# Retention, routed experts and a cosine layer on one core: paired scores, capacities by rank, paced transfers, a branch around the overflow turns

## The chip, the cores and the metric

The kernel runs on one core of a Trainium2 chip. The metric is the device time of one execution in microseconds (us), as the median of several runs; lower is better. The engines are TensorE (PE; PEld is its weight load), VectorE (DVE), ScalarE (ACT), GpSimd (POOL) and SyncE (SP), each with its own instruction queue, worked through in order. SP starts most transfers, GpSimd the indirect ones.

## The reference

Three layers follow one another on 4 x 576 = 2304 tokens of 512 columns (8 heads of 64):

```
# 1. retention, per head, gamma = 1 - 2^(-5-h)
scores = q @ k.T / 8;  ret = scores * (gamma ** (i - j) where i >= j else 0);  x = ret @ v
# 2. top 2 of 8 experts; noisy = x @ w_gate + log1p(exp(x @ w_noise)) * noise
w = softmax of the two largest of noisy
out[token] += w_k * (relu(x @ w1[e]) @ w2[e])     # w1 512 x 1024, w2 1024 x 512
# 3. h = out @ w_in (512 x 2048);  result = (h * cos(h)) @ w_out (2048 x 512)
```

q, k, v, the gate and the experts are float32; the last layer's two weights arrive as float64. With the reference's own inputs the experts get 614, 587, 570, 539, 535, 566, 606 and 591 tokens.

## The kernel before

**Retention** goes tile by tile (20 tiles: four of 128 tokens and one of 64 in each batch). For tile j SP loads queries (`qr`), keys (`kb`) and keys and values (`kv`), four tiles ahead (`LOOK`). GpSimd multiplies queries and values by decays (`decay`, L418; `decay_v`, L426), VectorE the first four tiles' queries. `scores` (L444) makes K Q^T for eight heads: `kb` is held in two copies with one head's 64 rows set to zero, so that each matmul uses all 128 rows. VectorE masks the result out of PSUM (L445, two instructions of 128 x 512 a tile). `outputs` (L468 to L487) adds what the running state gives, multiplies with the values, the two heads of a pair on column halves of the array (L473), and renews the state. `gate` and `gate_t` make the routing logits and write the tokens to `xs` in DRAM in 32 x 32 blocks.

**Routing** runs in four groups of tiles (`routing`, a generator): softplus, the two largest, ranks by matmuls with ones, then a table of tokens by slot, built from one-hot tiles (`sa` L645, `sb` L646). `pump` hands its steps to VectorE between the steps of the array, by estimates (`spent`) of what array and VectorE were given so far, always the older group first (`LASTFIRST` is False). Expert 0's first 320 tokens (`CUT0`), known after two groups, are served early: `layer1(0, 0, True)` and `layer2(0, 0, True)` keep the array busy while routing ends (`fill`, and the loop over `post`).

**Experts.** Each has 616 slots (`CAP`), whatever its count; tokens beyond go through `overflow` in plain float32, 128 a turn, in a loop whose number of turns is loaded into registers at run time. Weights come in units of 128 x 1024 through three staging tiles (`load_unit`, SP). `split_unit` takes each into a float32r high part (ScalarE, L288) and a low part (L289, VectorE or GpSimd by lists as `B_POOL`, `SA_POOL`); both layers use three products, high-high, low-high and high-low (`PASSES`; L796 and L817). An expert's columns go in two groups (256 and 360; expert 0: 320 and 296). `gather` fetches the next expert's rows for blocks of 128 tokens by four indirect transfers each (L721, GpSimd), all of them issued ahead of the expert; `turn` transposes them by VectorE in 32 x 32 blocks (L754) and splits them. Results are turned back and go to `ys`. Beside this VectorE turns the float64 weights to float32 by their bits (`conv`, L1116 to L1122), in steps spread by `CG0`, `CG1` and `CG2`.

**Last layer.** Nine blocks of 256 tokens (the last 128 by halves): `fetch` (L1150, sixteen indirect transfers a block), `turn2` (weigh, add, transpose, split), `mlp1` (L1190 to L1208) and `mlp2` (L1220). A block's fetch runs during the block before it; the first block's during the last expert.

The order is written out by hand: the loops at the end of `moe_kernel` say after which step of the array each split, turn, gather and conversion step is put.

Of the kernel before, what the change touches and what calls it, by code (L numbers as in the profile page):

```python
# [10 lines left out]
F32 = mybir.dt.float32  # L11
# [20 lines left out]
# slots of an expert, in two groups: expert 0's and the others'  # L32
CAP = 616
NB = 5
CUT0, CUT = 320, 256
ROOM = (CUT0, CAP - CUT)
XB = (N - 512) // 128
YR = E * CAP
# [7 lines left out]
ZERO = (11, 13, 22, 27, 27, 29, 33)  # L46
LOOK = 4
WJ = 3
T0_AT = ()
GLP = 8  # L50
GLP0 = 4
FS = 1
FS0 = 1
SPP = (0, 3, 6, 9)
SP0 = (0, 1, 2, 3, 4, 5, 6, 7, 8, 9)
CG0 = 4
CG1 = 2
CG2 = 1
SB_AT = (1, 4, 7, 10)
SB_POOL = ()  # L60
SA_POOL = (1, 2, 3, 4, 5, 6)
TURN_AT = (1, 2, 3, 5, 6)
SPLIT_AT = (1, 2, 4, 5)
L_AT = (1, 2, 3, 5, 8, 9, 10, 11, 13, 15)
L_POOL = (2, 4, 7)
T2_AT = (1, 2)
# [6 lines left out]
LASTFIRST = False  # L73
# [3 lines left out]
L_US = 0.04  # L77
# [6 lines left out]
B_AT = (0, 1, 2, 24)  # L84
B_POOL = range(99)
TURN_AT0 = (1, 1, 2, 3, 4)
# [4 lines left out]
# where the last layer's weight units go: 8 of w_in, 8 of w_out  # L91
# [27 lines left out]
def constants():  # L119
# [26 lines left out]
    # counts from which an expert needs one, two, ... turns more  # L146
    xb = np.tile(512 + 128 * np.arange(XB), (E, 1))
    xb[:, 0] = CAP
# [8 lines left out]
    small = np.concatenate([xb, io, base, k[:, None], k[:, None] // 32, tok, it], 1)  # L157
    # k = 32 g + t to 32 a + t, for every a
# [9 lines left out]
SMALL = [("xb", E * XB), ("io", E), ("base", GN * E), ("pi", 1), ("pa", 1), ("tok", NTILE), ("it", E * RB)]  # L168
# [25 lines left out]
    # rows of tokens lie as [32-row of the array, chunk, 32]; expert 0's are turned a 128 at a time  # L194
# [19 lines left out]
def moe_kernel(ctx, tc, x, out, dbg=None, phases="ABC"):  # L214
# [29 lines left out]
    spread = be.tile([128, 4, 128], F32, name="spread")  # L244
    vs = con.tile([128, 2, NTILE], F32, name="vs")
    eix = con.tile([128, 2, NTILE], F32, name="eix")
    oh = con.tile([128, 2, NTILE, E], F32, name="oh")
    gidx = con.tile([128, E * RB], I32, name="gidx")
    egid = con.tile([128, 3], I32, name="egid")
    cnt = con.tile([128, E], F32, name="cnt")  # L250
    ntot = con.tile([128, 1], I32, name="ntot")
    cbias = con.tile([128, 2], F32, name="cbias")
    nc.gpsimd.memset(cbias[:, 0:1], MAGIC)
# [3 lines left out]
    units = []  # L257
    for e in range(E):
        units += [(f"a{j}", x["w1"][4 * (e or E) + j], [128, DC, 256]) for j in range(4)]
        units += [(f"b{j}", x["w2"][4 * e + j], [128, 2, DM]) for j in range(4)]  # L260
# [3 lines left out]
    state.update(load=0, split=0, a=wpa)  # L264
# [4 lines left out]
    def load_unit():  # L269
        u = state["load"]  # L270
        if u >= len(units):
            return
        state["load"] += 1
        st = stage.tile([128, 1024], F32, name="st")
        nc.sync.dma_start(st, units[u][1])
        loaded[u] = st

    def split_unit(lo_engine=nc.vector):
# [13 lines left out]
        load_unit()  # L292

# [8 lines left out]
    # the array's clock rises while it works: it is kept busy until the first data are there  # L302
# [11 lines left out]
    for i in range(LOOK):  # L314
        t = ca.tile([128, HP, 2, 128], F32, name=f"kb{i}")
        eng = nc.gpsimd if i else nc.vector
        eng.memset(t[:64, :, 1, :], 0.0)
        eng.memset(t[64:, :, 0, :], 0.0)
        KB.append(t)
# [10 lines left out]
    def load_k(j):  # L330
        b, c = divmod(j, NC)
        kb, src = (KB[(4 * b + c) % LOOK], x["kt"][4 * b + c]) if c < 4 else (KBT, x["ktt"][b])
        for s in range(2):
            nc.sync.dma_start(kb[s * 64:(s + 1) * 64, :, s, :],
                              src[s * 64:(s + 1) * 64].rearrange("p (a t) -> p a t", a=HP))
        KT[j] = kb
# [44 lines left out]
    adj = rt.tile([128, E], BF, name="adj")  # L381
    ptab = ps.tile([128, E * RB], F32, name="ptab")
    lgs = []
    for i in range(2):
        t = rt.tile([128, GN, 2 * E], F32, name=f"lg{i}")
        lgs.append(t)

    def late_consts():
# [18 lines left out]
        nc.sync.dma_start(spread.rearrange("p a b -> p (a b)"), x["c_spread"])  # L407
# [27 lines left out]
    def scores(j):  # L435
        b, c = divmod(j, NC)
        am = wk.tile([128, HP, 2, 128], F32, name="am", bufs=2)
        if c < 4:
            for h2 in range(2):
                p = ps.tile([128, 2, 2, 128], F32, name="ph", bufs=PHB)  # L440
                for i in range(2):
                    hp = 2 * h2 + i
                    for s in range(2):
                        nc.tensor.matmul(p[:, i, s, :], KT[j][:, hp, s, :], QT[j][:, hp, :], start=True, stop=True)  # L444
                nc.vector.tensor_tensor(  # L445
                    am[:, 2 * h2:2 * h2 + 2].rearrange("p a s q -> p (a s) q"),
                    p.rearrange("p a s q -> p (a s) q"),
                    bs["mask"][:, None, :].to_broadcast([128, 4, 128]), op=OP.mult)
                AM[j] = am
                yield  # L450
# [44 lines left out]
    def gate(j):  # L495
# [9 lines left out]
        # tokens to spread rows, 32 x 32 at a time  # L505
# [19 lines left out]
    def spread_out(src, tag, bufs):  # L525
        """[32 g + t, n] to [32 a + t, g, n] for every a."""
        n = src.shape[-1]
        pq = ps.tile([128, 4, n], F32, name=tag, bufs=bufs)
        for g in range(4):
            nc.tensor.matmul(pq[:, g], spread[:, g], src, start=True, stop=True)  # L530
        return pq

    ranked, begun = [0], []
# [801 lines left out]
```

## Time and profile before

| | |
|---|---|
| median of three runs | 1105.34 us (1099.04 to 1111.32) |
| span of the profiled execution, first to last instruction | 1012.0 us (its time with what lies around is not given) |
| TensorE / its weight loads busy | 970.4 / 912.4 us |
| VectorE / ScalarE / GpSimd busy | 699.4 / 369.6 / 532.1 us |
| mean granted clock of TensorE | 0.988 of full speed |
| moved by DMA | 135.4 MB, 134 GB/s over the span |

Busy times are sums over each engine; the span is longer than any of them. "Idle before" belongs to the instruction behind it, with what ended it in brackets. Granted clock 1.00 is full speed, 2.4 GHz.

### The profile page before, as it was taken

The page shows a single profiled execution, that of the slowest core. Times are in us where ns is not written, and L with a number is a line of the kernel's source. Part 1 is how long each engine was busy: PE and PEld are TensorE (multiplying, and loading weights), DVE is VectorE, ACT ScalarE, POOL GpSimd, SP SyncE. Part 2 cuts the span into 40 slices and gives each one's busy share as a digit, 9 for nine tenths or more (in the row PEclk, how much of TensorE's full clock was granted, in tenths as well). Part 3 has the DMA queues.
Part 4 walks back from the last instruction along what each step waited for, and adds up shares of the span by engine and source line. Part 5 has one row for each costly group of instructions (what it writes and reads, how often), then busy time and mean ns, then how long its engine had stood idle before and what let it go on. Part 6 is the DMA issues. An engine that isn't in the chain of part 4 may idle for free. (4 is left out here: it accounts for less than half of the span.)

```text
span 1012.0 us, 17885 instructions
## 1 busy us (share of the span) xinstructions
PE 970.4 (96%) x6845; PEld 912.4 (90%) x6845; DVE 699.4 (69%) x1337; ACT 369.6 (37%) x657; POOL 532.1 (53%) x467
## 2 busy tenths in 40 slices
PE   8989987989999999999999999899999999999998
PEld 6878777979999999999999998799898989989897
DVE  4698883697989889894444459585665848475671
ACT  2422411242323232233333336353443535354451
POOL 6343333676655647475731447374746456473721
PEclk9999988989999999999999999999999999999999
DMA  9999584275866768484525533101111010111100
GB/s 284 285 268 271 137 276 132 78 230 169 233 234 196 239 205 283 146 281 120 165 87 155 146 94 123 47 25 42 32 37 50 21 50 19 45 29 41 32 22 22
DMA packets 85847, 135.38 MB, mean 134 GB/s; under 512 B 13376, under 2 KB 51648, under 8 KB 85760
## 3 DMA queue, kind: packets, MB, share of 16 engines
q1 hardware_dynamic: 76048, 113.74, 36.5%
q0 software_dynamic: 9568, 20.20, 7.0%
q8 instruction: 55, 0.90, 0.4%
q10 hardware_dynamic: 144, 0.27, 0.1%
q14 instruction: 32, 0.26, 0.1%
HBM read 106.25 MB, written 35.26 MB: 140 GB/s over the span
## 5 line engine op out<-in xcount | busy, mean ns | idle before, releaser
L721 POOL DMA_INDIRECT rows<-xs,gidx x140 | 154.3, 1102 | 55.9 <-issue 46.6
L1150 POOL DMA_INDIRECT y<-ys,slot x144 | 141.0, 979 | 56.0 <-issue 26.1
L1208 POOL TENSOR_TENSOR gl<-t,gh 128x512 fp32r<-128x512 f32 x68 | 88.6, 1303 | 139.7 <-issue 110.1
L289 POOL TENSOR_TENSOR la<-st,ha 128x1024 fp32r<-128x1024 f32 x28 | 69.6, 2492 | 98.3 <-ACT ha L288 98.3
L817 PE MATMUL ph<-hh,lb 128*128 128x360 f32 (+2 forms) x312 | 96.0, 308 | 0.0
L817 PE MATMUL ph<-hl,hb 128*128 128x360 f32 (+2 forms) x312 | 95.9, 308 | 0.0
L817 PE MATMUL ph<-hh,hb 128*128 128x360 f32 (+2 forms) x312 | 95.5, 306 | 0.0
L1169 DVE SCALAR_TENSOR_TENSOR y<-y,wts,y 128x128 f32<-128x128 f32 x72 | 34.8, 511 | 61.6 <-DMA y<-ys,slot 54.6
L1198 DVE TENSOR_SCALAR t<-t 128x512 int32<-128x512 int32 x72 | 73.1, 1016 | 2.5
L1196 DVE TENSOR_SCALAR t<-t 128x512 f32<-128x512 f32 x72 | 37.4, 519 | 50.3 <-ACT t L1195 50.3
L746 ACT ACTIVATE xh<-xt 128x512 fp32r<-128x512 f32 (+1 forms) x35 | 21.5, 616 | 137.8 <-DVE xt L754 137.8
L1201 ACT ACTIVATE t<-t,cbias 128x512 f32<-128x512 f32 x72 | 52.0, 722 | 33.0 <-DVE t L1198 32.0
L1220 PE MATMUL py<-hd,gl 128*128 128x512 f32 (+1 forms) x152 | 57.7, 380 | 1.5 <-DVE gl L1208 1.5
L817 PEld LDWEIGHTS ph<-hh,hb 128*128 128x128 f32 x312 | 58.9, 189 | 0.0
L817 PEld LDWEIGHTS ph<-hl,hb 128*128 128x128 f32 x312 | 58.6, 188 | 0.0
L817 PEld LDWEIGHTS ph<-hh,lb 128*128 128x128 f32 x312 | 58.5, 188 | 0.0
L1220 PE MATMUL py<-hb,gl 128*128 128x512 f32 (+1 forms) x152 | 58.4, 384 | 0.0
L1220 PE MATMUL py<-lb,gh 128*128 128x512 f32 (+1 forms) x152 | 58.4, 384 | 0.0
L1220 PE MATMUL py<-hb,gh 128*128 128x512 f32 (+1 forms) x152 | 58.3, 384 | 0.0
L1220 PE MATMUL py<-hd,gh 128*128 128x512 f32 (+1 forms) x152 | 57.5, 378 | 0.0
L1220 PE MATMUL py<-ld,gh 128*128 128x512 f32 (+1 forms) x152 | 57.5, 378 | 0.0
L796 PE MATMUL ph<-xh,ha 128*128 128x360 f32 (+3 forms) x236 | 45.8, 317 | 6.3 <-DVE hl L802 4.3
(309 smaller groups left out, 2705.5 us busy)
## 6 DMA issues: line engine op xcount, KB each, us to landing
st<-w SPq DMA_DIRECT2D x64, 512.0 KB
kv<-kv SPq DMA_DIRECT2D x16, 512.0 KB
ci<-wi SPq DMA_DIRECT2D x16, 512.0 KB
wc<-cy SPq DMA_DIRECT2D x32, 256.0 KB
ci<-wo SPq DMA_DIRECT2D x16, 512.0 KB
st<-wc SPq DMA_DIRECT2D x16, 512.0 KB
ys<-c_zero SPq DMA_DIRECT2D x7, 1024.0 KB
qr<-qt SPq DMA_DIRECT2D x20, 256.0 KB
```

Source lines behind the costliest of these rows:

```text
L289: lo_engine.tensor_tensor(lo.rearrange("p a b -> p (a b)"), st, hi.bitcast(F32).rearrange("p a b -> p (a b)"), op=OP.subtract)
L721: nc.gpsimd.indirect_dma_start(out=t[:, g, :], out_offset=None, in_=xs.rearrange("n (a d) -> (n a) d", a=4), in_offset=bass.IndirectOffset ...
L746: nc.scalar.activation(hi, src, AF.Copy)
L796: nc.tensor.matmul(p[:, :n], w[a][:, dc, (f % 2) * 128:(f % 2 + 1) * 128], XE[e, g][b][:, dc, :n], start=(i == 0), stop=(i == 3 * DC - 1))
L817: nc.tensor.matmul(p[:, :n], w[a][:, f % 2, c * 128:(c + 1) * 128], HE[e, g][b][:, f, :n], start=(i == 0), stop=(i == 3 * FC - 1))
L1150: nc.gpsimd.indirect_dma_start(out=t[:, g, :], out_offset=None, in_=(ys if i else ys[:FIRST]).rearrange("n (a d) -> (n a) d", a=4), in_off ...
L1169: nc.vector.scalar_tensor_tensor(y0[:, g], y1[:, g], w1, y0[:, g], op0=OP.mult, op1=OP.add)
L1196: nc.vector.tensor_scalar(t, t, -MAGIC, None, op0=OP.add)
L1198: nc.vector.tensor_scalar(t.bitcast(I32), t.bitcast(I32), 0x7FFFFFFF, None, op0=OP.bitwise_and)
L1201: nc.scalar.activation(t, t, AF.Sin, scale=-1.0, bias=cbias[:, 1:2])
L1208: (nc.gpsimd if g < (GLP if i else GLP0) else nc.vector).tensor_tensor(fl(gl), T[g], fl(gh.bitcast(F32)), op=OP.subtract)
L1220: nc.tensor.matmul(ps_[tb][:, :c1 - c0], parts[f // 2][b][:, f % 2, tb * 128:(tb + 1) * 128], w[a][:, f % 2, c0:c1], start=(f + k == 0), s ...
```

## The change

Keys lie in one piece and each head's scores use half of the array's rows, two heads side by side into two PSUM banks. Experts 1 to 7 are served in the order of their counts, with capacities from 616 down to 560 (`CAPS`); expert 0 stays first. For that `rank_experts` sorts counts on VectorE behind the last group's table, and SP loads seven expert numbers into registers; the weights of experts 1 to 7 are addressed by them, and loads asked for before are owed. The last routing group's steps go first, and the end of the earlier groups is put off (`rest`). The two of seven 1 MB zero writes to `ys` that were issued during retention move behind it. Most low parts go from GpSimd to VectorE, at other places. GpSimd takes the gathers one by one, each behind a one-element copy of the array's last result (`pace`). Expert 1's first two blocks and the last layer's first block are fetched as whole rows, one transfer a block and source, and transposed by TensorE. The overflow loop stands in a branch. Expert 0's early group has 352 columns.

```diff
-CAP = 616
+CAPS = (616, 616, 600, 592, 584, 576, 568, 560)
+BASE = tuple(sum(CAPS[:i]) for i in range(E))
-CUT0, CUT = 320, 256
+CUT0, CUT = 352, 256
-ZERO = (11, 13, 22, 27, 27, 29, 33)
+ZERO = (22, 27, 27, 29, 33, 38, 44)
-LASTFIRST = False
+LASTFIRST = True
-L_US = 0.04
+L_US = 0.1
-B_AT = (0, 1, 2, 24)
-B_POOL = range(99)
+B_AT = (0, 5, 10, 24)
...
 def load_unit():
+        if u // 8 < E and u // 8 not in expert:
+            state["owed"] += 1
+            return
...
 def scores(j):
-            for h2 in range(2):
-                p = ps.tile([128, 2, 2, 128], F32, name="ph", bufs=PHB)
-                for i in range(2):
-                    hp = 2 * h2 + i
-                    for s in range(2):
-                        nc.tensor.matmul(p[:, i, s, :], KT[j][:, hp, s, :], QT[j][:, hp, :], start=True, stop=True)
...
+            pp = [ps.tile([128, HP, 128], F32, name="ph", bufs=PHB) for _ in range(2)]
+            for hp in range(HP):
+                for s in range(2):
+                    h = slice(s * 64, s * 64 + 64)
+                    nc.tensor.matmul(pp[s][:, hp, :], KT[j][h, hp, :], QT[j][h, hp, :], start=True, stop=True)
+            for s in range(2):
+                nc.vector.tensor_tensor(am[:, :, s, :], pp[s], bs["mask"][:, None, :].to_broadcast([128, HP, 128]),
+                                        op=OP.mult)
...
+    def rank_experts():
...
+        vec.tensor_copy(cnt, pn)
+        vec.scalar_tensor_tensor(key, cnt, 8.0, sl["tie"], op0=OP.mult, op1=OP.add)
+        vec.tensor_tensor(sq, row(key), column(key), op=OP.is_gt)
+        vec.tensor_reduce(at_, sq, axis=AX.X, op=OP.add)
+        vec.tensor_tensor(hot, row(at_), column(sl["io"]), op=OP.is_equal)
+        vec.tensor_tensor(sq, hot, row(sl["io"]), op=OP.mult)
+        vec.tensor_reduce(order, sq, axis=AX.X, op=OP.add)
+        for e in range(1, E):
+            expert[e] = nc.values_load(order[0:1, e:e + 1], engines=[mybir.EngineType.SP], min_val=1, max_val=E - 1)
+        for _ in range(state["owed"]):
+            load_unit()
...
 def routing(gi):
...
+            yield from rank_experts()
+            vec.tensor_tensor(gs, hot[:, :, None, :].to_broadcast([128, E, NB, E]),
+                              gf.rearrange("p e n -> p n e")[:, None].to_broadcast([128, E, NB, E]), op=OP.mult)
+            vec.tensor_reduce(gf, gs, axis=AX.X, op=OP.add)
+            vec.tensor_copy(whole, gf[:, 1, :WHOLE1])
...
+    def pace(src):
+        nc.gpsimd.tensor_copy(beat, src.bitcast(F32))
...
 def turn(e, blk, early=False):
+            if e:
+                t = bpool[1].tile([128, DC, 128], F32, name="xt")
+                nc.scalar.activation(t.rearrange("p c (a d) -> p c a d", a=4),
+                                     ROWS[e, blk].rearrange("p a (c d) -> p c a d", c=DC), AF.Copy)
             for a in range(4):
-                nc.tensor.transpose(p[:, a, :], ROWS[e, blk][:, a, :], ident)
+                nc.tensor.transpose(p[:, a, :], t[:, a, :], ident)
...
 def pump():
+            elif m == "done" and not l1:
+                gens.remove(it)
+                rest.append(it)
...
-            split_unit(nc.gpsimd if k in B_POOL else nc.vector)
-            if k not in B_POOL:
-                spent(0, B_US)
+            split_unit()
+            spent(0, B_US)
...
 def overflow():
         total = nc.values_load(ntot[0:1, 0:1], min_val=0, max_val=OVB)
-        with tc.tile_pool(name="ov", bufs=1) as ov:
+        with tc.If(total > 0):
+            with tc.tile_pool(name="ov", bufs=1) as ov:
...
 # the order of the experts
+        gq = gathers(e + 1) if e + 1 < E else iter(())
+        if not e:
+            steps(gq, WHOLE1)
...
             for _ in layer1(e, g):
                 n += 1
+                pace(HE[e, g][0][0:1, (n - 1) % FC, 0:1])
+                steps(gq, 2 if last and n < 13 else 1)
...
-                elif state["split"] < 8 * e + 8 and n in SB_AT:
-                    split_unit(nc.gpsimd if n in SB_POOL else nc.vector)
-                if not e or n > CG0 and n % CG1 == 0:
+                elif n in ((*SB_AT, *SA_AT) if e else SA_AT0):
+                    split_unit()
+                if not e or n in CG_1:
                     steps(cg, 1)
...
 # the order of the last layer
             if n in SP0 and state["split"] < len(units):
-                split_unit(nc.gpsimd if n in SPP else nc.vector)
-            steps(fg, FS if i else FS0)
+                split_unit()
+            if not i and parts:
+                pace(parts[-1][0][0:1, 0, 0:1])
+            steps(fg, 1 if i or n > 5 else 2)
```

## Rows read from the trace of the kernel before

**Rows 1.** Busy times by stage: length, engines' busy us (instructions), granted clock, DMA share, GB/s.
```profile
20.00:106.00 86.00, 78.48 (x812) 68.01 (x810) 69.23 (x214) 27.63 (x63) 36.43 (x39) 1.00 0.94 274
...
122.00:168.40 46.40, 35.20 (x241) 32.60 (x240) 30.23 (x113) 9.37 (x19) 12.34 (x7) 0.89 0.63 197
168.40:217.50 49.10, 44.07 (x295) 43.45 (x296) 34.82 (x70) 14.71 (x27) 33.56 (x27) 0.89 0.44 130
217.50:594.00 376.50, 373.76 (x2595) 371.41 (x2593) 275.74 (x471) 121.06 (x205) 210.99 (x158) 1.00 0.60 189
...
645.20:1012.00 366.80, 363.26 (x2352) 332.35 (x2352) 225.57 (x341) 160.70 (x281) 188.18 (x174) 1.00 0.12 34
sum 1012.00, PE 970.40 PEld 912.44 DVE 699.43 ACT 369.65 POOL 532.08; mean PE 121.30 PEld 114.06 DVE 87.43 ACT 46.21 POOL 66.51
```

**Rows 2.** The chain that ended last: start, us, what; 256 columns, then 512.
```profile
645.24 4.38 PE ptab L1190 x24
...
670.00 22.15 PE py L1220 x96
...
697.89 5.76 PE pt L1190 x48
```

**Rows 3.** Timeline of TensorE in one tile of retention: start, us, instruction, count.
```profile
45.50 2.05 PE L444 MATMUL ph<-qt,kb 128*128 128x128 f32 x16 [0.94 <-POOL qt L418]
...
48.93 1.09 PE L473 MATMUL py<-am,vt 128*64 128x128 f32 x16
```

**Rows 4.** Waits of all engines: total us, times, longest.
```profile
POOL qt L418 <- DMA qr<-qt: 37.6, 10, 7.5
```

**Rows 5.** Groups of VectorE's instructions from 20 to 122 us.
```profile
L445 DVE TENSOR_TENSOR am<-ph,cb 128x512 f32<-128x512 f32 x27 | 17.9, 679 | 0.6 <-PE ph L444 0.4
```

**Rows 6.** Timeline of three engines around 130 us.
```profile
125.38 7.04 POOL L289 TENSOR_TENSOR lb<-st,hb 128x1024 fp32r<-128x1024 f32 x3 [10.93 <-ACT hb L288]
130.09 2.38 DVE L645 TENSOR_SCALAR sa<-it,vf 128x128 f16<-128x128 f16 x1
132.62 0.24 DVE L645 TENSOR_SCALAR sa<-it,vf 128x128 f16<-128x128 f16 x1
133.54 1.44 PE L796 MATMUL ph<-xh,ha 128*128 128x320 f32 x4 [4.29 <-DVE hl L802]
137.71 0.91 PE L796 MATMUL ph<-xh,ha 128*128 128x320 f32 x4
```

**Rows 7.** Groups of the whole span: the low parts of weight units.
```profile
L289 POOL TENSOR_TENSOR la<-st,ha 128x1024 fp32r<-128x1024 f32 x28 | 69.6, 2492 | 98.3 <-ACT ha L288 98.3
L289 DVE TENSOR_TENSOR lb<-st,hb 128x1024 fp32r<-128x1024 f32 x29 | 36.2, 1248 | 5.6 <-ACT hb L288 5.3
```

**Rows 8.** Timeline of TensorE behind the overflow loop.
```profile
168.44 1.35 PE L796 MATMUL pt<-xh,ha 128*128 128x296 f32 x4 [6.28 <-DMA ys<-y]
...
172.41 0.71 PE L796 MATMUL pt<-xh,la 128*128 128x296 f32 x4
```

**Rows 9.** Timeline of TensorE at the start of expert 1.
```profile
206.24 1.16 PE L796 MATMUL ph<-xh,la 128*128 128x256 f32 x4 [1.84 <-POOL la L289]
...
209.76 0.65 PE L796 MATMUL ph<-xl,ha 128*128 128x256 f32 x4
...
213.20 1.22 PE L796 MATMUL pt<-xh,ha 128*128 128x256 f32 x4 [2.79 <-DVE hl L802]
```

**Rows 10.** Timeline: expert 0's last gathers on GpSimd, transposes on TensorE.
```profile
152.24 0.95 POOL L726 DMA_INDIRECT rows<-xs,gidx  x1 [0.30 <-issue]
153.49 0.95 POOL L726 DMA_INDIRECT rows<-xs,gidx  x1 [0.30 <-issue]
160.69 1.03 PE L763 MATMUL pt<-ident,rows 128*128 128x128 f32 x8
```

**Rows 11.** Timeline of TensorE in the last layer's first block and behind it.
```profile
630.56 0.50 PE L1220 MATMUL py<-hd,gl 128*128 128x512 f32 x1 [1.51 <-DVE gl L1208]
...
645.24 0.74 PE L1190 MATMUL ptab<-x2h,hc 128*128 128x256 f32 x4 [3.85 <-ACT x2h L746]
```

More of the change, by code (lines that the diff above doesn't have):

```diff
@@ L1 @@
 from contextlib import ExitStack
+from functools import partial
 from itertools import chain
@@ L257, in moe_kernel, with unit @@
     units = []
+    expert = {0: 0}
+    def unit(name, e, j):
+        if not e:
+            return x[name][4 * (E if name == "w1" else 0) + j]
+        return x[name][bass.ds(expert[e] * 4 + j, 1)].rearrange("u p c -> (u p) c")
     for e in range(E):
-        units += [(f"a{j}", x["w1"][4 * (e or E) + j], [128, DC, 256]) for j in range(4)]
-        units += [(f"b{j}", x["w2"][4 * e + j], [128, 2, DM]) for j in range(4)]
+        units += [(f"a{j}", partial(unit, "w1", e, j), [128, DC, 256]) for j in range(4)]
+        units += [(f"b{j}", partial(unit, "w2", e, j), [128, 2, DM]) for j in range(4)]
     wcf = wc.bitcast(F32)
@@ L263, in moe_kernel @@
     loaded, W = {}, {}
-    state.update(load=0, split=0, a=wpa)
+    state.update(load=0, split=0, owed=0, a=wpa)
     def x_tiles(g):
@@ L381, in moe_kernel @@
     adj = rt.tile([128, E], BF, name="adj")
+    hot = rt.tile([128, E, E], F32, name="hot")
+    order = rt.tile([128, E], I32, name="order")
     ptab = ps.tile([128, E * RB], F32, name="ptab")
@@ L386, in moe_kernel, with drain @@
         lgs.append(t)
+    def drain(g):
+        for _ in g:
+            pass
     def late_consts():
@@ L651, in routing @@
         yield "table"
+        while tabled[0] < gi:
+            yield "wait"
+        tabled[0] += 1
         table(0, gi == len(GRP) - 1)
@@ L713, in moe_kernel, with spread_rows, gathers @@
     ROWS, XE, HE, bpool = {}, {}, {}, {0: be}
+    def spread_rows(e, blk):
+        return e > 1 or e == 1 and blk >= WHOLE1
+    def gathers(e):
+        for blk in range(NB):
+            yield from gather(e, blk)
     def gather(e, blk, early=False):
@@ L836, in layer2 @@
         yield
-    gens, clock, early = [], [0], []
+    gens, rest, clock, early = [], [], [0], []
     at = {"P": 0.0, "D": 0.0}
@@ L877, in pump_to @@
                 return
+            elif m == "done" and len(gens) > 1:
+                rest.append(gens.pop(0))
+        for it in rest[::-1]:
+            drain(it[0])
     turned = []
@@ L1146, in fetch @@
             ys12 = []
+            if not i:
+                for kk in range(2):
+                    t = cx.tile([128, 4, 128], F32, name=f"y{kk}", bufs=2)
+                    nc.gpsimd.indirect_dma_start(out=t.rearrange("p a d -> p (a d)"), out_offset=None, in_=ys[:FIRST],
+                                                 in_offset=bass.IndirectOffsetOnAxis(ap=slot0[:, kk, j:j + 1], axis=0))
+                    yield
+                    ys12.append(t)
+                Y12[i].append((j, *ys12))
+                continue
             for kk in range(2):
@@ L1252, in moe_kernel @@
     for e in range(E):
-        if e + 1 < E:
-            for blk in range(NB):
-                gather(e + 1, blk)
+        gq = gathers(e + 1) if e + 1 < E else iter(())
+        if not e:
+            steps(gq, WHOLE1)
         n = 0
@@ L1276, in moe_kernel @@
                     drain(layer2(e, 0))
-                    drain(fetch(0))
+                    gq = fetch(0)
         t2 = turn2(0) if last else iter(())
         m = 0
+        if 0 in T2_AT:
+            steps(t2, 1)
         for _ in chain(layer2(e, 0), layer2(e, 1)) if 0 < e < E - 1 else layer2(e, 1):
             m += 1
+            steps(gq, 2 if last or not e else 1)
             if last:
@@ L1290, in moe_kernel @@
                         turn(e + 1, blk)
-                if m in SPLIT_AT or not e:
-                    split_unit(nc.gpsimd if m in SA_POOL else nc.vector)
-            steps(cg, CG2)
+                if state["split"] < 8 * e + 12:
+                    split_unit()
+            if e and m in CG_2:
+                steps(cg, 1)
         if e == E - 2:
```

353 lines of the change are left out of this document (203 added, 150 removed).

## The prediction

> **What bounds the kernel now.** I read the busy times by stage first, then the chain of waits, then the timeline of TensorE wherever a stage was not full, and last the groups of instructions for the durations. TensorE works 970.4 of 1012.0 us. The stages [rows 1] are retention and gate (20 to 106, running out by 122), the routing of the last tokens with expert 0's early product as filler (to 168.4), expert 0's second group and the start of expert 1 (to 217.5), experts 1 to 7 (to 594), the first block of the last layer (to 645), and the eight other blocks. The expert stage (373.8 of 376.5 us) and the last stage (363.3 of 366.8) are full: there only fewer matmul columns help. The other four lack 7.5, 11.2, 5.0 and, by its two idles [rows 11], 5.4 us, and in two of them the mean granted clock is 0.89: after a long idle TensorE comes back at the lower of its two levels (1.2 instead of 2.4 GHz) for a few us. What is won there is the idle time and the slow stretch behind it. In retention the DMA share is 0.94 while TensorE is 91% and VectorE 80% busy, so three resources are near their end together.
>
> The chain ends in nothing but matmuls of the last layer, so what is saved ahead of them moves the end one to one. The sum is made against the span of the one profiled execution; no time of its own is given for it. The median of the runs, 1105.3 us, is 93.3 above that span; I keep these 93.3.
>
> **The change, part by part.**
>
> *Ranked capacities.* 4,928 expert columns (8 x 616) become 4,712, so 216 fewer. A column passes 192 matmuls (96 in each layer of an expert: 8 x 4 x 3). A matmul of 256 columns takes 5.76/48 = 0.120 us, one of 512 22.15/96 = 0.231 [rows 2], so 0.432 ns a column. 216 x 192 x 0.432 ns = **17.9 us less**, all in the full stage. The bounds are close together: it comes out unless another engine takes over. It holds as long as no expert has more tokens than its slots, since no overflow turn runs before, and by the reference's own inputs the counts (614 for expert 0; then 606, 591, 587, 570, 566, 539, 535) fit the new capacities too.
>
> *Row-tiled scores.* Now 16 instructions with half the rows zero take 2.05 us a tile; the 16 that already go in pairs, on column halves, take 1.09 [rows 3]. If row halves pair as well, TensorE is given back 0.96 us x 16 tiles = 15.4 us; if not, nothing. It is not the only bound: GpSimd waits 37.6 us for the queries' transfers [rows 4], and TensorE then for GpSimd. What DMA gives back is the two 1 MB zero writes that leave this stage: 274 GB/s at a share of 0.94 is 291 at full, so 3.6 us each, 7.2 of 0.94 x 86 = 80.8 us. At the same share the stage then takes 73.6/0.94 = 78.3, 7.7 less. With about 1 us in the two tiles that run out behind it I take **8.5 us less**, between 0 and 15.4. VectorE's 69.2 us then stand in some 78 (88%): tight, but open. Keys in one piece instead of two save SP queue time and eight clears at the start; nothing on the path.
> A rule speaks against this step. VectorE reads the scores of a tile out of PSUM in two pieces of 0.68 us [rows 5], 1.36 us, more than the 1.09 that the paired matmuls would need. The Trainium skill says so in general (TensorEngine Tiling (Array Packing), PSUM Bottleneck): packing speeds up the array but not the emptying of PSUM, which may become the bottleneck. By it a tile would gain 2.05 - 1.36 = 0.69, 11 us in all; still above what the transfers allow, so my term stands.
>
> *Splits off GpSimd, and the order of routing.* At 125.4 GpSimd splits three weight units, 7.04 us. Meanwhile VectorE's routing instructions take up to 2.38 us instead of 0.24, and TensorE waits 4.29 us for VectorE [rows 6]. From there the next twelve matmuls of 320 columns, with four small ones between, take 4.17 us; at 0.148 each and 0.5 for the four it would be 2.3, so 1.9 more. That is 6.2 us. With these splits on VectorE (1.25 us each [rows 7]) and the last group's steps first, most of it goes: **5 less**; ends 6.2 less and, if the four splits fall into the routing chain itself, 5 more. What is late next is that chain; its cover is expert 0's early product, 10% longer now (352 instead of 320 columns, paid back in the second group).
>
> *Overflow in a branch.* The loop of zero turns costs an idle of 6.28 us and a slow stretch, 16 matmuls of 296 columns in 3.97 us [rows 8] where 0.137 each makes 2.2, so 1.8 more: 8.1. The register load and the jump on all engines remain, the loop's entry and exit should not. No row shows a branch alone; between 8.1 less and a second such idle, 6.3 more, I take **3 less**.
>
> *Expert 1.* TensorE idles 1.84 us for GpSimd's split and 2.79 for VectorE there, and 16 matmuls of 256 columns behind the first take 3.52 us [rows 9] instead of 1.92, 1.6 more; I put the same behind the second. That is 7.8 us. Splits earlier and on VectorE, and two blocks gathered as whole rows (1 indirect transfer in place of 4, 1.25 us apart): **5.5 less**.
> Against it stands the ranking: about 15 more VectorE instructions (0.2 to 0.5 us, some 5 us) and seven register loads on SP before any weight of expert 1 is asked for, with SP's queue behind them. The three gathers of expert 0 go out before; now 6 us lie between them and the end of the filler at 160.7 [rows 10], and expert 0's second group (24 us) comes still before expert 1. I take **2 more**; ends 0 and 8.8, seven times the 1.25 us that lie between two indirect transfers on their queue [rows 10], the nearest row to a load that a queue makes itself.
>
> *Last layer's first blocks.* 1.51 and 3.85 us of idle [rows 11]; behind the second 24 matmuls take 4.38 us [rows 2] instead of 2.88, 1.5 more: 6.9. Block 1's sixteen fetches go out two at a step and GpSimd loses its splits: **5 less**; ends 6.9 less, and 2.6 more if the splits on VectorE push its chain.
>
> *Added.* 16 transposes (8 take 1.03 us [rows 10]): **2 more**. One-element copies that pace GpSimd: 0, GpSimd is half idle; if its queue ran behind, expert turns would wait, which the gathers' slack (20 in 24 steps) excludes in the common case.
>
> Sum: -17.9 - 8.5 - 5 - 3 - 5.5 + 2 - 5 + 2 = -40.9. The span becomes 971, the time **1064 us**.
>
> **Rivals.**
> (a) *The ranking takes the place of the waits it stands beside*: steps 3 and 5 give nothing (10.5) and the register loads cost some 8 in front of expert 1. For it: weights can't be prefetched over it. Against: 24 us of cover. 1064 + 18 = 1082.
> (b) *Retention does not shrink*: the row halves do not pair (then the change does not do what it says), or VectorE or the transfers hold the pace. 1064 + 8.5 = 1073.
> (c) *VectorE becomes the bound of the experts*. The 28 splits that the row groups [rows 7] x 1.25 = 35 us come to its 341 us between 122 and 594 [rows 1]: 376 of about 445, 84%, and it loses the blocking by GpSimd. Only bursts could bind. The whole column gain would go: 1064 + 18 = 1082.
> (d) *Slower: TensorE's clock falls in retention.* With 13 us of scores taken out and the transfers as they are, it idles more often. Its price: work at the lower level takes twice as long, so the stage's 65 us of work could cost up to 65 more, 1129. It outweighs the gains from 41 us at the lower level on, that is from two thirds of the stage. Against it: this stage already idles 7.5 of 86 us in pieces and its granted clock is 1.00 [rows 1]; the falls named above follow idles of 1.8 us or more, and TensorE's waits here are of 1.3 at most.
>
> **How the numbers follow.** Forecast 0.62, (a) 0.17, (b) 0.09, (c) 0.06, (d) 0.06. The range takes in (a) to (c) and the better ends, 17.9 + 15.4 + 6.2 + 8.1 + 7.8 + 6.9 - 2 = 60 less, 1045; with some us of the runs' own spread (1099 to 1111) I give 1042 to 1090. One per cent, about what can be told from no change here, is 11 us: below 1094 is faster. That holds in the forecast, (b), and most of (a) and (c): 0.87; the same 0.08; slower 0.05, (d).
>
> **What would show it.** Expert matmuls of 344 down to 304 columns and an expert stage some 15 us shorter with VectorE below 90%; score pairs in 1.1 us a tile; retention's DMA share still above 0.9 with TensorE near 83%; no idle over 2 us before expert 0's late group except at the branch; a first fetch of block 1 done before its block 0 ends. I am wrong if TensorE waits for VectorE in the experts, for the weights of expert 1, or if retention still ends near 122.

## The result and the profile after

The changed kernel takes 956.24 us (954.50 to 959.04, four runs) against 1105.84 (1099.04 to 1111.32, four runs) before: a ratio of 0.868 [0.864, 0.873], 150 us less. Ratios, here and below, are estimated without runs over 1.5% above the fastest of the same kernel, with a 95% interval in brackets, so they need not equal the quotient of two medians. The forecast was 1064, with a range of 1042 to 1090; the sign was right, the size far off. In the profiled execution the changed kernel's span is 954.6 us and its time 956.36, so 1.8 us lie around the span, not the 93.3 that I kept. From span to span the change is worth 57.4 us, where my sum had 40.9.

So there are two questions: what the 93 us were, and where another 16 us of span came from. The page of the kernel after, first lines and three groups (line, engine, operation, count, busy us, mean ns, idle time ahead of them):

```profile
span 954.6 us, 18171 instructions
...
PE 935.2 (98%) x6861; PEld 878.1 (92%) x6861; DVE 676.1 (71%) x1381; ACT 367.8 (39%) x653; POOL 469.2 (49%) x536
...
L811 POOL DMA_INDIRECT rows<-xs,gidx x132 | 135.1, 1024 | 32.4 <-issue 25.3
L824 POOL COPY beat<-hh 1x1 f32<-1x1 f32 x120 | 49.0, 408 | 150.8 <-ACT hh L903 148.3
L311 DVE TENSOR_TENSOR lb<-st,hb 128x1024 fp32r<-128x1024 f32 x35 | 43.7, 1247 | 11.7 <-ACT hb L310 10.5
```

Ahead of the pacing copies GpSimd waits 150.8 us, 148.3 of them for ScalarE, and GpSimd is still only 49% busy. Stages of the kernel after (columns as in [rows 1]):

```profile
20.00:106.00 86.00, 79.80 (x886) 66.91 (x882) 71.12 (x227) 29.26 (x68) 39.26 (x43) 0.94 0.81 251
...
122.00:151.00 29.00, 27.71 (x192) 25.57 (x190) 21.36 (x98) 4.09 (x8) 4.78 (x5) 1.00 0.95 326
151.00:178.00 27.00, 24.79 (x200) 24.40 (x201) 21.18 (x73) 10.10 (x20) 14.55 (x20) 1.00 0.67 200
178.00:217.50 39.50, 39.50 (x298) 39.50 (x297) 28.96 (x51) 16.53 (x28) 24.76 (x36) 1.00 0.63 184
217.50:542.00 324.50, 324.36 (x2410) 324.15 (x2409) 246.41 (x468) 108.31 (x182) 152.63 (x201) 1.00 0.67 202
542.00:590.00 48.00, 46.04 (x291) 41.16 (x290) 38.43 (x59) 26.41 (x43) 29.63 (x30) 1.00 0.36 104
```

From 178 to 542 us TensorE has hardly a gap: the stage that lacked 5 us at expert 1 [rows 1] is full. Most of what is left ahead of the last layer is in retention (clock 0.94) and behind the branch. TensorE's timeline, start, us, instruction, idle before:

```profile
51.55 1.16 PE L478 MATMUL ph<-qt,kb 64*128 64x128 f32 x16
...
57.68 2.15 PE L478 MATMUL ph<-qt,kb 64*128 64x128 f32 x16 [2.12 <-DVE sa L721]
...
113.11 0.75 PE L898 MATMUL ph<-xh,ha 128*128 128x352 f32 x3 [0.27 <-ACT xh L842]
...
151.11 0.72 PE L898 MATMUL pt<-xh,ha 128*128 128x264 f32 x4 [0.43 <-PEq L1087]
...
154.72 0.75 PE L898 MATMUL pt<-xh,ha 128*128 128x264 f32 x4 [1.92 <-ACTq L1087]
...
178.03 0.64 PE L898 MATMUL pt<-xh,ha 128*128 128x256 f32 x4
...
589.88 0.74 PE L1337 MATMUL ph<-x2h,hc 128*128 128x256 f32 x4 [1.42 <-ACT x2h L842]
```

The profile puts the wait ahead of 57.68 down to `sa`, which these matmuls don't read. They read `qt`, and GpSimd made that after a wait for the queries' transfer, ready 0.06 us before they start, so the wait is most likely for that transfer:

```profile
56.36 1.26 POOL L452 TENSOR_TENSOR qt<-qr,dq 128x512 f32<-128x512 f32 x1 [4.13 <-DMA qr<-qt]
```

Read the starts. Expert 0's early product goes on behind the last gate at 113.11 (before 120.80), its late group starts at 151.11 (168.44 [rows 8]), expert 1 at 178.03 (197.38), the last layer at 542.06 (594.07), its block 1 at 589.88 (645.24 [rows 11]). The gains are 7.7, 9.6, 2.0, 32.7 and 3.4 us, and 2.0 in the eight blocks behind. Expert 0's 32 columns that moved from its late to its early group lie in the second and the third of these gains: by 0.432 ns a column they are 2.7 us, against the 9.6 and for the 2.0.

### The profile page after: what moved, and what is told of

Read it like the earlier page. It is cut to its first block, busy times and chain, and to the rows that moved or that the text cites. A ratio compares the mean times of both kernels' runs of the same rounds, so it can differ in the third digit from the quotient of the medians.

```text
span 954.6 us, 18171 instructions
## 1 busy us (share of the span) xinstructions
PE 935.2 (98%) x6861; PEld 878.1 (92%) x6861; DVE 676.1 (71%) x1381; ACT 367.8 (39%) x653; POOL 469.2 (49%) x536
## 4 chain that ended last, share of the span: by engine, by line
PE 79%; DVE 3%; issue 1%; ACT 1%; DMA 1%; DVEq 0%; SPq 0%; ACTq 0%
PE py L1366 19%; PE ph L919 13%; PE ph L1337 11%; PE ph L898 8%; PE pt L1337 7%; PE pt L898 7%; PE pt L919 4%; PE ptab L898 4%; PE ptab L1337 3%; PE ptab L919 3%; DMA st<-w 1%; DVE y L1316 0%; DVE t L1344 0%; DVE t L1349 0%; DVE hl L904 0%
## 5 line engine op out<-in xcount | busy, mean ns | idle before, releaser
L811 POOL DMA_INDIRECT rows<-xs,gidx x132 | 135.1, 1024 | 32.4 <-issue 25.3
L1280 POOL DMA_INDIRECT y<-ys,slot x128 | 125.7, 982 | 50.8 <-issue 21.1
L824 POOL COPY beat<-hh 1x1 f32<-1x1 f32 x120 | 49.0, 408 | 150.8 <-ACT hh L903 148.3
L919 PE MATMUL ph<-hl,hb 128*128 128x256 f32 (+8 forms) x304 | 91.0, 299 | 0.0
L919 PE MATMUL ph<-hh,lb 128*128 128x256 f32 (+8 forms) x304 | 91.0, 299 | 0.0
L919 PE MATMUL ph<-hh,hb 128*128 128x256 f32 (+8 forms) x304 | 90.7, 298 | 0.0
L1343 DVE TENSOR_SCALAR t<-t 128x512 f32<-128x512 f32 x72 | 35.0, 487 | 48.4 <-ACT t L1342 48.4
L1345 DVE TENSOR_SCALAR t<-t 128x512 int32<-128x512 int32 x72 | 67.1, 932 | 2.5
L842 ACT ACTIVATE xh<-xt 128x512 fp32r<-128x512 f32 (+7 forms) x33 | 19.6, 593 | 114.2 <-DVE xt L850 95.3
L1366 PE MATMUL py<-ld,gh 128*128 128x512 f32 (+1 forms) x152 | 57.4, 378 | 0.0
L311 DVE TENSOR_TENSOR lb<-st,hb 128x1024 fp32r<-128x1024 f32 x35 | 43.7, 1247 | 11.7 <-ACT hb L310 10.5
```

The source lines that it names most:

```text
L311: lo_engine.tensor_tensor(lo.rearrange("p a b -> p (a b)"), st, hi.bitcast(F32).rearrange("p a b -> p (a b)"), op=OP.subtract)
L811: nc.gpsimd.indirect_dma_start(out=t[:, g, :], out_offset=None, in_=xs.rearrange("n (a d) -> (n a) d", a=4), in_offset=bass.IndirectOffset ...
L824: nc.gpsimd.tensor_copy(beat, src.bitcast(F32))
L919: nc.tensor.matmul(p[:, :n], w[a][:, f % 2, c * 128:(c + 1) * 128], HE[e, g][b][:, f, :n], start=(i == 0), stop=(i == 3 * FC - 1))
L1280: nc.gpsimd.indirect_dma_start(out=t[:, g, :], out_offset=None, in_=ys.rearrange("n (a d) -> (n a) d", a=4), in_offset=bass.IndirectOffset ...
L1345: nc.vector.tensor_scalar(t.bitcast(I32), t.bitcast(I32), 0x7FFFFFFF, None, op0=OP.bitwise_and)
```

## The experiments

The kernel before was timed beside each. Its own level turned out to depend on the occasion, so each result is given with it. Rows of a trace are from one profiled execution of each kernel.

**The loop of overflow turns, put in a branch or taken out of it.** The first thought for the 93 us was the loop.

```diff
 # before
+        with tc.If(total > 0):   # around the overflow turns
 # after
-        with tc.If(total > 0):
```

> The kernel before, with nothing changed but the overflow loop put into a branch that is taken only when there are turns. Theory A (the 93 us that lie around the span of before belong to the loop that stands in no branch): the time falls by some 92 us to about 1014 or less, with about 2 us around the span; the idle behind the loop (6.28 us) shrinks too. Rival B (they belong to something else that the change removed: the loads of weights by fixed address, the split keys, the indirect transfers): the time stays at 1097 to 1106, the span loses at most the 8 us of the idle and its slow stretch. Rival C (the profiled execution of before was only a luckier one than the timed ones): no change in time, and a span near 1100.

> The changed kernel with the overflow loop in no branch, as before. Theory A: the time rises from 956 by 90 to 100 us to about 1050, the span by at most 6 us. Rival B: 956 to 962, with 2 us around the span. Rival C: 956 to 962.

Measured: 1007.6 with the branch against 1017.0 for before (0.992 [0.990, 0.994]); 956.5 for after with the loop, as after itself (956.2). Before itself took 1012 to 1028 us here, its span plus 1.8. In the traces the branch takes the idle behind the loop from 6.28 to 1.19 us; after with the loop has 5.84 there, and no time is lost by it that shows. In the kernel before the branch is worth up to 9 us, and on this occasion there was no 93 us to explain.

**Capacities of 616 for all.**

```diff
-CAPS = (616, 616, 600, 592, 584, 576, 568, 560)
+CAPS = (616,) * 8
```

> The changed kernel with 616 slots for every expert, ranked all the same: 216 columns more. By the matmul's 0.432 ns a column the time rises by 17.9 us to 974, if the array stays the bound of the experts; clearly less would mean that another engine had held the pace of the narrower experts already.

Measured 973.4 (968.8 to 975.5), 17 us above after; my term was 17.9. In the trace the stage from expert 1 to the last layer takes 382.6 us, with ranked capacities 364.0.

**Scores of one row half after those of the other, in the kernel after.**

```diff
-            for hp in range(HP):
-                for s in range(2):
+            for s in range(2):
+                for hp in range(HP):
```

> The changed kernel with the same score matmuls in another order: the four of one row half, then the four of the other, so that neighbours need the same rows and cannot go side by side. If pairing is what gives the array time back, 16 instructions take about 2 us again and not 1.16, 14 us more of TensorE's work in retention; theory A' (retention is held by TensorE): the time rises by 8 to 14 us, to 964 to 970. Rival (transfers and VectorE hold retention): it rises by under 4 us.

Measured 956.2 (953.5 to 959.8): no difference. The sixteen matmuls of a tile do get longer, row of that kernel's timeline:

```profile
53.05 1.71 PE L478 MATMUL ph<-qt,kb 64*128 64x128 f32 x16
```

So the pairing of row halves is real (1.16 us against 1.71), and in the kernel after it does not show in the time. In this profiled execution, the longest of the four, the early product goes on at 118.60 instead of 113.11 and the span is 3.4 us longer; what makes up for it in the others isn't shown.

**The kernel before again.**

> The kernel before, unchanged, once more. Its runs so far fall into two levels: 1099 to 1111 us in the comparison with the changed kernel, 1012 to 1028 us on the chip of the first experiments, while the changed kernel took 954 to 959 us beside both. Theory (d1), the level belongs to the chip or the occasion: all its runs here lie at one level, 1017 or 1105, and where they lie at 1105 the span is about 1103 with the rows of one stage longer by some 90 us. Theory (d2), the kernel falls into it execution by execution: both levels come here. Either way only 1.8 us should lie around the span, so my term of 93 us kept around the span is gone.

Measured 1015.96 (before beside it 1015.13). One level, 1.8 us around the span.

**Zero writes back in retention.**

```diff
-ZERO = (22, 27, 27, 29, 33, 38, 44)
+ZERO = (11, 13, 22, 27, 27, 29, 33)
```

> The kernel after with the zero writes put back where the kernel before has them, two of 1 MB inside retention (tiles 11 and 13). Theory (transfers bound retention): each costs 3.6 us of the 16 DMA engines, so retention's last gate comes up to 7 us later than at 112.4 and the time is 956 + 5 to 7 = 961 to 963. Rival (TensorE and VectorE bind there now, the transfers have slack): within 1 us of 956.

Measured 950.9 (950.5 to 952.6), where before took 1015. Both expectations miss: the two writes do not lengthen retention (the DMA share rises from 0.81 to 0.89, the early product goes on at 109.63; in after and seven runs of variants whose retention and zero writes were not edited, at 110.22 to 113.93), and in the routing stage the transfers have room again (share 0.74 instead of 0.95):

```profile
122.00:151.00 29.00, 25.95 (x173) 24.10 (x172) 20.69 (x91) 4.03 (x9) 4.77 (x5) 1.00 0.74 248
```

That room is not what the 5 us are: from the early product to the late group the two traces take 37.9 and 38.0 us. Of the 5.8 us of span between them, 3.5 are there by the early product and 1.6 are in the last layer. Why is open.

**Splits on GpSimd again, in the kernel after.**

```diff
-            split_unit()              # routing stage, and second layers
+            split_unit(nc.gpsimd)
```

> The kernel after with the splits of the routing stage and of the experts' second layers on GpSimd again. Theory (GpSimd's splits hold up VectorE): the stall of TensorE in the routing stage comes back (4.29 us of idle and 1.9 of slow matmuls before), the wait for GpSimd at expert 1 too (1.84 us and 1.6), in all 962 to 966. Rival (the other order of the routing steps hides them): 956 to 958.

Measured 957.1 (955.5 to 959.1). The stall is back in the trace, and the stretch from the early product to expert 0's late group takes 43.4 us instead of 38.0, which is the forecast's term of 5:

```profile
122.10 1.54 PE L898 MATMUL ph<-xh,ha 128*128 128x352 f32 x4 [5.07 <-DVE hl L904]
```

The wait at expert 1 did not come back. And in this execution retention had ended 2.7 us sooner, and in the last layer block 1 did not wait (409.7 us from its first matmul to the end, 412.5 in after's trace). In the time it does not show, as the rival had it.

**Row halves and keys in one piece, in the kernel before; then with the halves in turn.** The edits are the lines of the change in `load_k` and `scores`; the second run has the loops the other way round, as above.

> The kernel before with the row-tiled scores and the keys in one piece alone. Theory (retention shrinks by what the transfers let it): the two zero writes stay, so less than the 9.5 us by which the changed kernel's retention is shorter: 1 to 5 us below before, at about 1013 on the chip where before takes 1017. Rival (TensorE is the bound of retention): 10 us or more below, 1007 or less. Rival (the clock falls): nothing or slower.

> The kernel before with the keys in one piece and half-row scores, as in the run that took 11 us off it (1004.2 against 1015.1), but the four matmuls of one row half are issued before those of the other, so that pairs of row halves don't stand side by side. Theory (the pairing of row halves gave the 11 us): most of it goes again, scores about 1.75 us a tile instead of 1.16, 9 us of TensorE, so 1011 to 1014. Rival (the keys in one piece, with half as many loads and no clears, gave it): 1004 to 1006. The second rival on the level of 1105 us: if this chip shows the kernel before at 1105 again, its span says where.

Measured 1004.2 against 1015.1 (0.990 [0.987, 0.994]), 11 us less; in turn 1009.8 against 1016.1 (0.995 [0.992, 0.998]), 6 less. What the pairing gives by these two, 5 us, is hardly clear of the noise: the intervals overlap, on two occasions. The stage of retention, paired and then in turn, and the start of the early product in each:

```profile
20.00:106.00 86.00, 79.29 (x881) 66.10 (x880) 73.15 (x228) 29.43 (x68) 40.20 (x44) 0.96 0.87 277
20.00:106.00 86.00, 83.19 (x904) 71.08 (x905) 67.57 (x230) 30.52 (x71) 41.67 (x44) 1.00 0.85 276
111.67 0.71 PE L795 MATMUL ph<-xh,ha 128*128 128x320 f32 x3 [0.16 <-ACT xh L745]
111.83 0.71 PE L795 MATMUL ph<-xh,ha 128*128 128x320 f32 x3 [0.16 <-ACT xh L745]
```

Both end retention 9 us sooner than before (120.80, and up to 124.40 in five more profiles with before's retention), with all zero writes where they were, and the pairing makes no difference there. In turn, with 1.71 us a tile, TensorE is busy for 83.2 of 86 us; paired, with 1.16, it waits 2.0 us, most likely for the queries (the profile says `sa`, as above), and 2.5 us for VectorE's routing steps, and its clock falls to 0.96. The two spans differ by 2.9 us, all of it behind the early product.

What both runs share is scores in 1.71 us or less instead of 2.05, keys in one piece, and a smaller estimate of a tile's scores, by which `pump` hands out the routing steps. Keys in one piece lighten the transfers: 277 GB/s go at a DMA share of 0.87, where before needs 0.94 for 274 [rows 1], and GpSimd waits 23.6 and 24.5 us for the queries' transfers instead of 37.6 [rows 4] (31.5 at the least in those five profiles). No run has one of the three alone, so which of them gave the 9 us, and whether TensorE or the transfers held the pace of the kernel before, stays open.

**Experts in fixed order, 616 slots.**

```diff
-    expert = {0: 0}
+    expert = {e: e for e in range(E)}
-        for e in range(1, E):
-            expert[e] = nc.values_load(order[0:1, e:e + 1], ...)
```

> The kernel after with 616 slots for every expert, as in the run that took 973.4 us, and the experts in a fixed order: the ranking still computes its tables, but no weight waits for it and SP loads no register. The column saving is left out. Theory (the ranking is hidden behind expert 0's second group): 972 to 975, no difference from 973.4. My forecast's term: 2 us less, 971. Rival (a) of the prediction (the register loads cost about 8 us in front of expert 1): 963 to 967.

Measured 973.0 against 973.4 with the ranking, on another occasion: it is hidden. And here, minutes after the run before it and on the same chip, the kernel before took 1076 to 1088 us.

**The kernel before, caught at that level.**

> The kernel before, unchanged, a third time, to get a profile of its slow level. Beside the run with the fixed order it took 1076 to 1088 us at a mean granted clock of 0.957 to 0.969, a few minutes after 1014 to 1021 us at 0.980 to 0.988 on the same chip, so the level belongs to the occasion and not to the chip. Theory (t): on such an occasion its transfers are slower, and retention, where the DMA share is 0.94, is what gets longer, TensorE falling to its lower level in the waits: at 1078 retention's last gate comes some 60 us later than at 122. Rival (u): the loss is spread over the whole span, through the expert stage as well, as from a clock that is granted less: then every stage is 6 to 9% longer. If the occasion is a quick one, 1013 to 1018 and nothing is learnt.

Measured 1083.7 (1077.2 to 1094.8), 1088.2 beside it. This profile shows the missing time. Busy times on its page:

```profile
PE 997.2 (93%) x6845; PEld 925.3 (86%) x6845; DVE 695.8 (65%) x1337; ACT 367.7 (34%) x657; POOL 528.9 (49%) x467
```

TensorE's waits for issue (total us, times, longest):

```profile
PE ph L796 <- issue: 17.2, 21, 2.4
PE pt L796 <- issue: 15.9, 22, 2.4
PE ph L817 <- issue: 5.3, 8, 1.8
PE ptab L796 <- issue: 0.4, 1, 0.4
```

A stretch of the timeline of GpSimd and TensorE:

```profile
185.20 0.94 POOL L721 DMA_INDIRECT rows<-xs,gidx  x1 [0.30 <-issue]
185.59 0.65 PE L796 MATMUL pt<-xh,ha 128*128 128x296 f32 x2 [1.11 <-issue]
186.44 0.94 POOL L721 DMA_INDIRECT rows<-xs,gidx  x1 [0.30 <-issue]
186.99 0.41 PE L796 MATMUL pt<-xh,ha 128*128 128x296 f32 x1 [0.75 <-issue]
187.69 0.94 POOL L721 DMA_INDIRECT rows<-xs,gidx  x1 [0.31 <-issue]
188.42 0.59 PE L796 MATMUL pt<-xh,ha 128*128 128x296 f32 x1 [1.02 <-issue]
```

The waits for "issue" are waits for nothing that the profile shows; the profile of before at 1012.0 us has none. They add up to 38.8 us, and TensorE's busy time is 26.8 us longer (997.2 against 970.4): together, within 0.2, the 65.4 us by which this span, 1077.4, exceeds 1012.0. The mean granted clock over the span is 0.966 instead of 0.988, so most of the longer busy time can be work at the lower level: an estimate from the two means is 24 us. 63.8 of the 65.4 us lie behind the overflow loop and ahead of the last layer: expert 0's late group takes 45.7 us instead of 28.9, the experts 443.7 instead of 396.7, the last layer 416.9 instead of 417.9. So theory (t), retention's transfers, is out, and (u), every stage longer, too. And the long rows of such waits (182 to 200, 532 to 547, 648 to 653) lie where GpSimd issues gathers (in the last row the last layer's fetches) 1.25 us apart without a pause; TensorE's matmuls then come 0.7 or 1.4 us apart.

**Pacing put into the kernel before, taken out of the kernel after, and the loop against it.** These four runs decide.

```diff
 # before, with pacing alone
-        if e + 1 < E:
-            for blk in range(NB):
-                gather(e + 1, blk)
+        gq = gathers(e + 1) if e + 1 < E else iter(())
...
             for _ in layer1(e, g):
                 n += 1
+                pace(HE[e, g][0][0:1, (n - 1) % FC, 0:1])
+                steps(gq, 1)
 # after, without it
     def pace(src):
-        nc.gpsimd.tensor_copy(beat, src.bitcast(F32))
+        pass
```

> The kernel before with one part of the change alone: the gathers of the next expert go out one at a time, each behind a one-element copy that waits for a step of expert layer 1, not 20 in a row. In the slow execution of before (1077.4 us of span) TensorE waits 38.8 us for nothing that the profile shows, in stretches in which GpSimd issues indirect gathers 1.25 us apart without a pause, and its matmuls then come 0.7 or 1.4 us apart; in the quick one (1012.0 us) the same rows of gathers cost it nothing. Theory (p, rows of gathers hold up TensorE's instructions on some occasions): where the kernel before takes 1077 to 1090 here, this one takes 1010 to 1025, with hardly a wait for issue; where before takes 1016, this one takes 1013 to 1020. Rival (q, the loop of zero overflow turns does it): as before on either occasion, within 10 us.

> The kernel after without the pacing copies: GpSimd runs ahead and issues the gathers in a row again. Theory (p): where before takes 1077 to 1090 here, this one takes 980 to 1020, with waits for issue behind the gathers; where before takes 1016, 953 to 960. Rival (q): 953 to 960 on either. My forecast's term (the copies cost nothing and bring nothing): 956.

> The kernel after with the loop of zero turns in place of the branch, once more, for an occasion on which before is slow. Theory (p): 954 to 960, as on the quick occasion (956.5). Rival (q): 980 to 1050 where before takes 1077 to 1090.

> The kernel before with the branch around the overflow turns, once more. Theory (p): 9 us below before on either occasion, so 1068 to 1080 where before takes 1077 to 1090. Rival (q): 1005 to 1012 on either.

On this occasion before took 1101.8 us (1090.9 to 1112.3). Before with pacing: 1023.5 (two runs; 0.926 [0.917, 0.936]), 78 us less (76 without the runs left out of the ratios) and within 9 of its level on other occasions. After without pacing, its gathers still one by one in the program: 1013.6 (two runs), 53 above the 960.3 of after with the loop. Before with the branch: 1100.4, no different. So pacing decides and the loop does not. TensorE's waits for issue, in after without pacing, and then in before with it:

```profile
PE ph L919 <- issue: 11.8, 20, 1.1
PE ptab L919 <- issue: 6.6, 10, 1.0
PE pt L898 <- issue: 6.0, 7, 2.4
PE ph L898 <- issue: 5.0, 5, 1.8
...
```

```profile
PE pt L810 <- issue: 6.4, 1, 6.4
PE ph L831 <- issue: 4.5, 6, 1.0
```

The 6.4 in the second is the stop behind the overflow loop, which has another name here. Nearly all of the rest, from 588 to 595 us, lies beside fetches of the last layer, which are not paced in that kernel.

**Copies that wait for nothing.**

```diff
-        nc.gpsimd.tensor_copy(beat, src.bitcast(F32))
+        nc.gpsimd.tensor_copy(beat, cbias[0:1, 0:1])
```

> The kernel after with the pacing copies still between the gathers, but reading a constant, so that they wait for nothing. Tells apart two readings of the pacing. Reading (r1, the wait does it: what hurts is gathers issued far ahead of the array's steps): where before takes 1077 to 1110, this takes 990 to 1015, as without the copies (1013.6). Reading (r2, the pause between gathers does it, some 0.5 us of other work): 954 to 965. Where before takes 1016 both give 953 to 960 and nothing is learnt.

Measured 999.2 (989.8 to 1002.4), with before at 1109.4: the time of reading (r1). But the gathers are hardly further apart, and the waits are there (start, us, of GpSimd and TensorE):

```profile
157.32 0.97 POOL L811 DMA_INDIRECT rows<-xs,gidx  x1 [0.16 <-issue]
158.29 0.18 POOL L824 COPY beat<-cbias 1x1 f32<-1x1 f32 x1
158.63 0.97 POOL L811 DMA_INDIRECT rows<-xs,gidx  x1 [0.16 <-issue]
...
163.74 0.28 PE L898 MATMUL ph<-xh,ha 128*128 128x264 f32 x1 [1.06 <-issue]
```

A copy of 0.18 us that waits for nothing is not enough. That it must wait for the array is not shown by this: by the starts in the traces the median gap between gathers is 1.32 us here, 1.25 without copies and 1.62 in the kernel after, and a longer pause without a wait was not tried.

**Zero writes earlier, where before takes 1109 us.**

> The kernel after with the zero writes where the kernel before has them, which took 950.9 us where before took 1015. If it is a better version on any occasion, 948 to 956 here too, where after takes 954 to 959; rival: on an occasion on which before takes 1077 or more the earlier transfers cost something, 956 to 965.

> The kernel after with all zero writes earlier still: four of 1 MB inside retention (tiles 7, 9, 11, 13), the other three by step 9 of the routing stage. Theory (transfers have slack in retention and are short in the routing stage, where the DMA share was 0.95): 948 to 951, as with two in retention or a little less. Rival (four are too many, the queries come late): 955 to 962.

Two writes in retention (the edit above): 955.9 (954.8 to 957.6), with before at 1109.4. Four, `ZERO = (7, 9, 11, 13, 22, 27, 29)`: 962.4 (960.8 to 962.6). Four are too many: retention's DMA share is 0.91 and TensorE waits up to 2.98 us for GpSimd's multiplied queries. Whether two beat the kernel after stays open: 950.9 on one occasion is below all that after took, 955.9 on another is not, and the two never ran side by side.

## Why the prediction was wrong

**The step that failed** is "I keep these 93.3", and with it "One-element copies that pace GpSimd: 0". A median 9% above the span was no fixed amount around the execution; it was TensorE waiting inside the expert stage, and working part of it at the lower clock, on occasions, in a way that the profile of an undisturbed execution could not show, and the pacing that I costed at nothing is what ends it. On such an occasion it measures 53 us (taken out of after) to 76 or 78 (put into before), and it is the largest single part of the 150. Why the waits come is not known. On the others before takes 1016 and the change is worth 60; pacing alone was not tried there. That the runs shown at first were of this kind is inferred: they have no profile, but they lie at the level of the 1091 to 1115 seen later, and no run shows more than 2.3 us around its span.

**Ranked capacities**, 17.9: right, 17.0 in time and 18.5 in the stage.

**Row-tiled scores**, 8.5: the stage gained 7.7 (up to 10.6 in variants of after with the same retention), but the way to it was wrong. I bounded the gain by the two zero writes that leave; with no write moved the kernel before gains 9, and with the two put back the kernel after loses nothing. And I put keys in one piece at "nothing on the path", by the queue's time and the clears alone; they lighten the transfers, and they are in every run that gained. My signs failed too: the DMA share was to stay above 0.9 with TensorE near 83%, and they are 0.81 and 93% (79.8 of 86). That the sum came near is luck. VectorE's emptying of PSUM did not hold the pace in the kernel after: VectorE is 71.1 of 86 us busy, and TensorE's waits put down to its two pieces of 0.68 us a tile come to 0.6 us. By the rule of the Trainium skill (TensorEngine Tiling (Array Packing), PSUM Bottleneck) the emptying may become the bottleneck behind packing; this trace does not bear that out. In the kernel after, rival (d) came in small: an idle of 2.12 us, most likely for the queries' transfer, and one of 2.70 us behind VectorE's routing steps, the tile behind the first at 2.15 us instead of 1.16, a clock of 0.94.

**Splits and routing order**, 5, **and the branch**, 3: 9.6 to the start of the late group, and 2.0 in that group, 11.7 where I had 8. No `sa` takes more than 1.26 us (2.38 [rows 6]), splits take 1.25 on VectorE, and the 5 came back in the trace, though not in the time, when they went back to GpSimd. Part of the branch's stop moved behind the first matmuls: 0.43 and 1.92 us in place of 6.28.

**Expert 1 and the ranking**, 5.5 less and 2 more: mis-sized. From expert 1 to the last layer the gain is 32.7, 18.5 of it columns. Of the other 14.2, idle time gives 7.6 (TensorE's gaps in that stage were 7.7 and are 0.2), and the slow stretch behind them about 3.4 (20.1 us at a mean clock of 0.83, now 1.00); the ranking costs nothing that can be measured, so rival (a) is out. Some 3 us have no owner. VectorE stays at 76% there, so rival (c) is out too.

**Last layer's first blocks**, 5: 3.4, with a wait of 1.42 us left at block 1 in place of 3.85 and a further 2.0 gained behind it.

Against the span the sum of 40.9 would have stood at 971, and it was 954.6; 13.3 of the 16.5 missing lie in the expert stage (32.7 against 17.9 + 5.5 - 2 - 2 = 19.4).

## What to carry to other kernels

When the profiled execution is much quicker than the median, the difference is a case of its own: ask which part of the change could touch it, and give it a chance and a price, in place of carrying it along. Look for an engine that runs far ahead in a row of transfers; making it wait for the consumer's steps may cost nothing and take out a loss that the profile of a quick execution doesn't show. And test a bound by taking the binding thing back: two writes put back into retention showed that the transfers of the kernel after had slack. An edit of two parts needs a run of each: the shorter scores and the keys in one piece came together, and their shares can't be told.

## What the hardware showed

On some occasions, on the same chip within minutes of others, rows of indirect gathers issued 1.25 us apart ahead of the array go with waits of TensorE for nothing the profile shows (38.8 us in one execution, its matmuls 0.7 or 1.4 us apart). It isn't the load on the DMA engines: from 180 to 205 us only the gathers move, with 12.3% of them:

```profile
q0 software_dynamic: 448, 0.92, 12.3%
```

Nor do the queues of instruction transfers move more than in the quick execution: 55 and 32 packets in both, 0.4 and 0.1% of the engines' time.

What TensorE lacks then, its instructions or something else, and what makes an occasion one or the other, is not settled. In the quick execution a row as close, 20 gathers from 168.9 us on, costs nothing.
